# One core, two attention layers and two MLPs, forward and backward: chunks of wo kept over passes, 4 KiB transfers, gradient products in four row groups, and zero writes between the backward loads

## The chip, the cores and the metric

The kernel runs on one core of one Trainium2 chip. The metric is the device time of one execution in microseconds (us), as a median of several executions. Each profile, and each stage time read from one, is of a single execution of its kernel. A ratio is the mean time of one kernel's runs over the mean of the other's of the same rounds, so it is not quite the ratio of the medians quoted beside it.

Engines in the profile: PE does matrix products, PEld is its weight load (it overlaps PE), DVE and ACT evict results from PSUM (the memory that PE's products go to) to SBUF (the working memory), POOL and SP issue transfers. "Chunk" below is one piece of a weight matrix, 128 partitions by 2048 (or 1792) bf16 numbers, about 0.5 MB, loaded into a ring of streaming buffers.

## The reference

One token, decode, batch 1, all in bf16: four layers A1, B2, A3, B4 with residuals. A and B are used twice with the same weights.

```python
def A(x):   # attention over the last 4096 of 32768 cached keys
    q = (x @ wq).reshape(1, 1, 32, 128)               # wq 1024 x 4096
    p = softmax(q @ k[last 4096] * 128**-0.5)         # 4 kv heads, 8 q heads each
    return (p @ v[last 4096]).reshape(1, 1, 4096) @ wo # wo 4096 x 1024
def B(x):   # MLP with mish
    return mish(x @ w1 + b1) @ w2                     # w1 1024 x 3584, w2 3584 x 1024
x = x + A(ln(x)); x = x + B(ln(x)); x = x + A(ln(x)); x = x + B(ln(x))
# outputs: x, and the gradients of x, k_cache, v_cache, wq, wo, w1, b1, w2
```

Three facts matter. Every weight of wo, w1 and w2 is read in each of the four passes that need it, forward as it is stored, backward transposed, and the transposes are made on PE. The gradients of the weights are sums of two outer products (two layers), so each is a product with a contraction of only 2. And the gradients of the two caches are zero outside the last 4096 positions: 56 MB of zeros must be written some time.

## The kernel before

Weights wq, K and V stay in SBUF; wo, w1 and w2 are streamed. SP issues loads and zero writes in program order; a load waits only for its buffer. All other engines are ordered at build time by a scheduler. The backward stream of the MLP, with seven buffers:

```python
NB = 7
strm = tile_pool(name="strm", bufs=NB)
...
def mlp_bwd(g_col, g_bf, lname, sv):
    for c in reversed(range(TF // 2)):                  # 14 chunks of w2
        w = strm.tile([P, 2, D], BF16, name="w2_c", tag="st")     # cut: last ones held from forward
        nc.sync.dma_start(w[:], w2_v[:, 2 * c:2 * c + 2, :])      # 2 KB runs
        for tt in range(2):
            xpose_unit(w[:, tt, :], 8)    # 8 PE transposes to PSUM, one eviction back over w
        for tt in range(2):
            for dch in range(TD):
                mm(dacc[:, t:t + 1], w[:, tt, dch * P:(dch + 1) * P], g_bf[:, dch:dch + 1], ...)
    ...                                                 # the same with 16 chunks of w1
```

The zeros go out in 1 MB jobs: ten in each forward attention (`if c == NB - 1: zeros(10)` in the loop over wo), and in the backward in two blocks:

```python
g3, g3b = mlp_bwd(gcol, gcol_bf, "B4", sB4)
g2, g2b = attn_bwd(g3, g3b, "A3", sA3, True)
zeros(16)
g1, g1b = mlp_bwd(g2, g2b, "B2", sB2)
g0, g0b = attn_bwd(g1, g1b, "A1", sA1, False)
zeros(100)                                              # what is left
```

The gradients come last. Columns are transposed to rows on PE, and a transfer from the POOL queue puts each row in the tile ROWS. One product, one eviction:

```python
to_row(sB4["a_bf"], TF, 96, 0, "a4") ; to_row(...) x3    # 4 row puts before each gradient
def dw_tall(base, r0, L, out_v, name):
    for rr in range(2):
        for i in range(2):
            mm(ps[:], ROWS[base:base + 2, ...128 columns], ROWS[base:base + 2, ...512 columns],
               True, True, tile_position=(base, 0))     # all of one gradient in one row group
            ev_out(st[:, rr, i * 512:(i + 1) * 512], ps[:])
    nc.gpsimd.dma_start(out_v[:, r0:r0 + 2, :], st[:])
```

Of the kernel before, what the change touches and what calls it, by code (L numbers as in the profile page):

```python
# [15 lines left out]
P = 128  # L16
# [3 lines left out]
NB = 7  # L20
# [4 lines left out]
def kernel(  # L25
# [44 lines left out]
    stage = ctx.enter_context(tc.tile_pool(name="stage", bufs=4))  # L70
    pt = ctx.enter_context(tc.tile_pool(name="pt", bufs=4, space=bass.MemoryType.PSUM))
    pbig = ctx.enter_context(tc.tile_pool(name="pbig", bufs=1, space=bass.MemoryType.PSUM))
    pacc = ctx.enter_context(tc.tile_pool(name="pacc", bufs=1, space=bass.MemoryType.PSUM))

# [21 lines left out]
    ZC = 512  # L96
# [8 lines left out]

    wq_v = A_wq.rearrange("(t p) j -> p t j", p=P)
    wo_v = A_wo.rearrange("(t p) d -> p t d", p=P)
    w1_v = B_w1.rearrange("(t p) f -> p t f", p=P)
    w2_v = B_w2.rearrange("(t p) d -> p t d", p=P)
# [5 lines left out]
    for out_t in (out_2, out_3):  # L115
        for g in range(G):
            zflat = out_t[0, g, 0:ZR, :].rearrange("(p r) d -> p (r d)", p=P)
            for i in range(per // (8 * ZC)):
                zero_jobs.append(zflat[:, i * 8 * ZC:(i + 1) * 8 * ZC].rearrange("p (r c) -> p r c", c=ZC))

    def zeros(n):
        for _ in range(min(n, len(zero_jobs))):
            nc.sync.dma_start(zero_jobs.pop(0), zt[:, None, :].to_broadcast([P, 8, ZC]))
# [11 lines left out]
    def xpose_unit(ap2d, nb):  # L135
        ps = pt.tile([P, 8, P], BF16, name="tps", tag="pt")
        for b in range(nb):
            nc.tensor.transpose(ps[:, b, :], ap2d[:, b * P:(b + 1) * P], ident_bf[:])  # L138
        evac(ap2d, ps[:, 0:nb, :].rearrange("p b c -> p (b c)"), 0.08 * nb, 0.12 * nb)

# [6 lines left out]
    def ln_fwd(x_col, name):  # L147
# [14 lines left out]
        n_bf = keep.tile([P, TD], BF16, name=f"nbf_{name}")  # L162
        nc.vector.tensor_scalar(out=n_bf[:], in0=x_col[:], scalar1=s12[:, 0:1], scalar2=rstd[:, 0:1], op0=ALU.subtract, op1=ALU.mult)
# [4 lines left out]
    def ln_bwd(dn_ps, n32, rstd, g_col, name):  # L168
# [14 lines left out]
        g_bf = keep.tile([P, TD], BF16, name=f"gbf_{name}")  # L183
        nc.vector.tensor_copy(g_bf[:], g_new[:])
# [17 lines left out]
    def xpose_kv(lst):  # L202
        for w in lst:
            flat = w[:].rearrange("p t d -> p (t d)")
            for u in range(TK // 8):
                xpose_unit(flat[:, u * 1024:(u + 1) * 1024], 8)

# [34 lines left out]
    def to_kpart(src, name):  # L242
# [3 lines left out]
        dst = work.tile([P, TJ, P], BF16, name="kpart")  # L246
# [3 lines left out]
    def attn_fwd(x_col, lname, first):  # L250
# [40 lines left out]
        o_bf = keep.tile([P, HQ], BF16, name=f"obf_{lname}")  # L291
        nc.vector.tensor_copy(o_bf[:], oacc[:])
        sv["o_bf"] = o_bf
        yacc = acc_tile(TD)
        for c in range(HQ // 2):
            w = strm.tile([P, 2, D], BF16, name="wo_c", tag="st")
            nc.sync.dma_start(w[:], wo_v[:, 2 * c:2 * c + 2, :])
            if c == NB - 1:
                zeros(10)
# [11 lines left out]
    def mlp_fwd(x_col, lname, last):  # L311
# [3 lines left out]
        for t in range(TD):  # L315
            for hf in range(2):
                w = strm.tile([P, F // 2], BF16, name="w1_c", tag="st", padded_shape=[P, 2048])
                nc.sync.dma_start(w[:], w1_v[:, t, hf * (F // 2):(hf + 1) * (F // 2)])
                for b in range(TF // 2):
                    fb = hf * (TF // 2) + b  # L320
                    mm(hacc[:, fb:fb + 1], w[:, b * P:(b + 1) * P], n_bf[:, t:t + 1], t == 0 and fb == 0, t == TD - 1)
# [13 lines left out]
        a_bf = keep.tile([P, TF], BF16, name=f"abf_{lname}")  # L335
        nc.vector.tensor_mul(a_bf[:], h[:], t_f[:])
        sv["a_bf"] = a_bf
        yacc = acc_tile(TD)
        for c in range(TF // 2):
            w = strm.tile([P, 2, D], BF16, name="w2_c", tag="st")  # L340
            nc.sync.dma_start(w[:], w2_v[:, 2 * c:2 * c + 2, :])
# [23 lines left out]
    def mlp_bwd(g_col, g_bf, lname, sv):  # L365
        sv["g_bf"] = g_bf
        dacc = acc_tile(TF)
        for c in reversed(range(TF // 2)):
            w = w2_held.pop(c, None)
            if w is None:  # L370
                w = strm.tile([P, 2, D], BF16, name="w2_c", tag="st")
                nc.sync.dma_start(w[:], w2_v[:, 2 * c:2 * c + 2, :])
# [8 lines left out]
        dh_bf = keep.tile([P, TF], BF16, name=f"dhbf_{lname}")  # L381
        nc.vector.tensor_copy(dh_bf[:], dh[:])
# [3 lines left out]
        for t in range(TD):  # L386
            for hf in range(2):
                w = strm.tile([P, F // 2], BF16, name="w1_c", tag="st", padded_shape=[P, 2048])
                nc.sync.dma_start(w[:], w1_v[:, t, hf * (F // 2):(hf + 1) * (F // 2)])
                for u in range(2):  # L390
                    xpose_unit(w[:, u * 896:(u + 1) * 896], 7)
# [3 lines left out]
        return ln_bwd(nacc[:], sv["n32"], sv["rstd"], g_col, lname)  # L395
# [8 lines left out]
    def attn_bwd(g_col, g_bf, lname, sv, first):  # L404
        sv["g_bf"] = g_bf
        dacc = acc_tile(HQ)
        for c in range(HQ // 2):
            w = strm.tile([P, 2, D], BF16, name="wo_c", tag="st")
            nc.sync.dma_start(w[:], wo_v[:, 2 * c:2 * c + 2, :])
            for tt in range(2):  # L410
                xpose_unit(w[:, tt, :], 8)
# [4 lines left out]
        pad, rep = pad_cols(dacc[:], 1.0, f"do_{lname}")  # L416
# [19 lines left out]
        dq_bf = keep.tile([P, HQ], BF16, name=f"dqbf_{lname}")  # L436
        nc.scalar.activation(dq_bf[:], qacc[:], ACT.Copy, scale=scale)
# [6 lines left out]
        return ln_bwd(nacc[:], sv["n32"], sv["rstd"], g_col, lname)  # L444

    ROWS = keep.tile([P, 5120], BF16, name="ROWS")

    def to_row(col_bf, n, part, off, name):
        ps = pt.tile([HQ, P], BF16, name="rw", tag="pt")
        nc.tensor.transpose(ps[0:n, :], col_bf[:, 0:n], ident_bf[:])  # L450
        rt = work.tile([HQ, P], BF16, name="rt", tag="rt", bufs=4)
        nc.vector.tensor_copy(rt[0:n, :], ps[0:n, :])
        nc.gpsimd.dma_start(ROWS[part:part + 1, off:off + n * P].rearrange("o (n p) -> o n p", p=P), rt[0:n, :])

    def col_out(col_bf, n, out_flat, name):
        ps = pt.tile([HQ, P], BF16, name="rw", tag="pt")
        nc.tensor.transpose(ps[0:n, :], col_bf[:, 0:n], ident_bf[:])
        rt = work.tile([HQ, P], BF16, name="rt", tag="rt", bufs=4)
        nc.vector.tensor_copy(rt[0:n, :], ps[0:n, :])
        nc.gpsimd.dma_start(out_flat.rearrange("(n p) -> n p", p=P), rt[0:n, :])  # L460

    oq = [0]

    def dw_psum(n=512):
        return pt.tile([P, 512], FP32, name="ops", tag="pt")
# [4 lines left out]
    def dw_wide(base, t, lo, width, nfree, out_ap, name):  # L470

        st = stage.tile([P, width], BF16, name="st_w", tag="so", padded_shape=[P, 2048])
        for i in range(width // nfree):
            ps = dw_psum()
            mm(ps[:, 0:nfree], ROWS[base:base + 2, t * P:(t + 1) * P], ROWS[base:base + 2, 1024 + lo + i * nfree:1024 + lo + (i + 1) * nfree],
               True, True, tile_position=(base, 0))
            ev_out(st[:, i * nfree:(i + 1) * nfree], ps[:, 0:nfree])
        nc.gpsimd.dma_start(out_ap, st[:])

    def dw_tall(base, r0, L, out_v, name):  # L480

        st = stage.tile([P, 2, D], BF16, name="st_t", tag="so")
        for rr in range(2):
            for i in range(2):
                ps = dw_psum()
                mm(ps[:], ROWS[base:base + 2, (r0 + rr) * P:(r0 + rr + 1) * P], ROWS[base:base + 2, L + i * 512:L + (i + 1) * 512],
                   True, True, tile_position=(base, 0))
                ev_out(st[:, rr, i * 512:(i + 1) * 512], ps[:])
        nc.gpsimd.dma_start(out_v[:, r0:r0 + 2, :], st[:])  # L489

    def dkv(x3, y3, x1, y1, out_t):
        ov = out_t[0, :, Sk - W:, :].rearrange("g (p t) d -> p g t d", p=P)
        for c in range(NC):
            for gp in range(2):
                st = stage.tile([P, 2, TJ, DH], BF16, name="st_kv", tag="so")
                for j2 in range(TJ // 2):
                    ps = dw_psum()
                    for jj in range(2):
                        j = 2 * j2 + jj
                        mm(ps[:, jj * 256:(jj + 1) * 256], x3[32 * c:32 * c + 32, j * P:(j + 1) * P],  # L500
                           y3[32 * c:32 * c + 32, 2 * gp:2 * gp + 2, :].rearrange("p g d -> p (g d)"), True, False, tile_position=(32 * c, 0))
                        mm(ps[:, jj * 256:(jj + 1) * 256], x1[32 * c:32 * c + 32, j * P:(j + 1) * P],
                           y1[32 * c:32 * c + 32, 2 * gp:2 * gp + 2, :].rearrange("p g d -> p (g d)"), False, True, tile_position=(32 * c, 0))
                    ev_out(st[:, :, 2 * j2:2 * j2 + 2, :].rearrange("p g t d -> p t g d"),
                           ps[:].rearrange("p (t g d) -> p t g d", t=2, g=2))
                nc.gpsimd.dma_start(ov[:, 2 * gp:2 * gp + 2, c * TJ:(c + 1) * TJ, :], st[:])


    x1, sA1 = attn_fwd(x0, "A1", True)
    b1_f = load_col(B_b1, TF, "b1")  # L510
    gcol = load_col(grad_out[0, 0, :], TD, "gcol")
    gcol_bf = keep.tile([P, TD], BF16, name="gcolb")
    nc.vector.tensor_copy(gcol_bf[:], gcol[:])
    x2, sB2 = mlp_fwd(x1, "B2", False)
    x3, sA3 = attn_fwd(x2, "A3", False)
# [3 lines left out]
    col_out(x4_bf, TD, out_0[0, 0, :], "o0")  # L519


    g3, g3b = mlp_bwd(gcol, gcol_bf, "B4", sB4)
    g2, g2b = attn_bwd(g3, g3b, "A3", sA3, True)
    zeros(16)
    g1, g1b = mlp_bwd(g2, g2b, "B2", sB2)
    g0, g0b = attn_bwd(g1, g1b, "A1", sA1, False)
    col_out(g0b, TD, out_1[0, 0, :], "o1")
    zeros(100)


    to_row(sB4["a_bf"], TF, 96, 0, "a4")
    to_row(sB2["a_bf"], TF, 97, 0, "a2")
    to_row(sB4["g_bf"], TD, 96, 4096, "g4")
    to_row(sB2["g_bf"], TD, 97, 4096, "g2")
    for t in range(0, TF, 2):
# [63 lines left out]
```

## Time and profile before

Median 654 us in three runs (653.41 to 654.88). The boundaries below are read from PE's timeline: forward ends where PE transposes the output, the backward parts end at their layernorm product (the first one of each), the gradients start with the last of these.

| stretch, us | before |
|---|---|
| forward: A1, B2, A3, B4 end at | 98.5, 138.4, 188.4, 225.6 |
| backward: B4, A3, B2, A1 end at | 272.6, 351.0, 403.7, 453.4 |
| end of the profiled span | 652.0 |

The page's row of 40 slices (16.3 us each; digits are tenths, PEclk is the TensorE clock granted, GB/s what the transfers moved):

```profile
PE   3564034465444599889978888866376979999696
...
PEclk9985555555555599989975999995555555555555
...
GB/s 307 425 415 383 388 286 390 388 386 383 388 387 392 252 281 333 296 283 382 382 390 153 289 288 298 304 384 382 384 390 195 289 185 309 218 195 139 153 224 292
```

Forward (slices 1 to 14) the transfers run mostly at 383 to 425 GB/s and PE is half idle: bound by DMA. In the backward streams (slices 15 to 28) PE is at 0.6 to 0.9, the clock mostly full, and the transfers move about 290 GB/s except where zeros fill in: bound by PE and its evictions. In the gradients (from slice 29) the clock is half and PE is busy again.

Busy time by windows. The columns are the window, its length, busy us (and count) of PE, PEld, DVE, ACT, POOL, then clock, DMA share and GB/s. The rows are B2 forward, the B4 backward, resident transposes, dV and dK:

```profile
99.00:138.00 39.00, 16.59 (x449) 14.24 (x449) 3.40 (x21) 0.72 (x3) 0.00 (x0) 0.50 1.04 393
...
226.00:270.00 44.00, 40.97 (x865) 36.66 (x864) 22.59 (x37) 22.46 (x24) 0.66 (x1) 0.96 0.84 288
...
303.00:329.00 26.00, 26.00 (x470) 26.00 (x468) 23.23 (x37) 22.23 (x24) 0.00 (x0) 1.00 1.09 383
...
561.00:585.00 24.00, 23.71 (x124) 16.30 (x125) 10.73 (x22) 9.38 (x16) 5.72 (x8) 0.50 0.48 175
587.00:612.00 25.00, 24.58 (x128) 16.74 (x128) 11.20 (x22) 9.80 (x17) 5.72 (x8) 0.50 0.44 160
```

And a piece of PE's timeline in the backward stream (start, duration, what, and in brackets an idle time before it, if any):

```profile
246.50 0.35 PE L145 MATMUL acc<-gcolb,w_c 128*128 128x1 bf16 x8
246.72 0.44 PE L138 MATMUL tps<-ident_bf,w_c 128*128 128x128 bf16 x5
246.99 0.34 PE L145 MATMUL acc<-gcolb,w_c 128*128 128x1 bf16 x8
247.20 0.66 PE L138 MATMUL tps<-ident_bf,w_c 128*128 128x128 bf16 x9
```

The transposes (tps) of one chunk and the products (acc) of the chunk ahead of it alternate in pieces of 5 to 9 and 8. While one chunk's transposes are evicted, PE has another chunk's work. No idle time is marked.

Before the gradients PE waits for rows (the list of PE's waits from 400 us on: total, times, longest):

```profile
PE ops L145 <- DMA ROWS<-rt: 26.3, 4, 10.8
```

### The profile page before, as it was taken

What the parts mean: (1) busy time and instruction counts of PE and PEld (TensorE: products, weight loads), DVE (VectorE), ACT (ScalarE), POOL (GpSimd) and SP (SyncE); (2) the same over time, 40 slices, a digit from 0 to 9 for tenths busy, and PEclk for the clock granted to TensorE, in tenths of its full rate; (3) what the DMA queues carried; (4) which work ended last, traced back from release to release, by engine and by line L of the source; (5) the groups of instructions that cost most, each with busy time, mean ns of one, the idle gap of its engine ahead of it and who ended that gap; (6) DMA issues with size and microseconds to landing.
All of it is one profiled execution on the core that took longest, in us unless ns stands there. A gap on an engine that the chain in (4) does not pass through costs nothing. (4 is left out here: it accounts for less than half of the span.)

```text
span 652.0 us, 16240 instructions
## 1 busy us (share of the span) xinstructions
PE 451.2 (69%) x7117; PEld 325.0 (50%) x7117; DVE 242.1 (37%) x470; ACT 203.4 (31%) x292; POOL 62.3 (10%) x109
## 2 busy tenths in 40 slices
PE   3564034465444599889978888866376979999696
PEld 2444023353433497778967777746121323466431
DVE  1140000102001055546842454431254757644275
ACT  1030000000000055446821444420253747443274
POOL 0000000000000000000000000000233334322322
PEclk9985555555555599989975999995555555555555
DMA  8999999999999689989994889999995748553457
GB/s 307 425 415 383 388 286 390 388 386 383 388 387 392 252 281 333 296 283 382 382 390 153 289 288 298 304 384 382 384 390 195 289 185 309 218 195 139 153 224 292
DMA packets 118215, 205.10 MB, mean 315 GB/s; under 512 B 11514, under 2 KB 68992, under 8 KB 117120
## 3 DMA queue, kind: packets, MB, share of 16 engines
q1 hardware_dynamic: 107328, 164.13, 70.5%
q0 software_dynamic: 10816, 39.94, 16.0%
q8 instruction: 55, 0.90, 0.5%
q14 instruction: 16, 0.13, 0.1%
HBM read 105.39 MB, written 98.58 MB: 313 GB/s over the span
## 5 line engine op out<-in xcount | busy, mean ns | idle before, releaser
L145 PE MATMUL ops<-ROWS 2*128 2x512 bf16 (+1 forms) x248 | 104.8, 606 | 29.8 <-DMA ROWS<-rt 26.3
L145 PEld LDWEIGHTS <-w_c 128*128 128x128 bf16 x1792 | 60.2, 101 | 67.3 <-DMA w_c<-in_B_w_dram 40.5
L145 PEld LDWEIGHTS <-ROWS 2*128 2x128 bf16 x248 | 33.6, 137 | 99.7 <-issue 88.9
L138 PE MATMUL tps<-ident_bf,w_c 128*128 128x128 bf16 x896 | 72.1, 225 | 0.0
L133 ACT COPY w_c<-tps 128x896 bf16<-128x896 bf16 (+1 forms) x48 | 45.8, 955 | 79.7 <-PE tps L138 74.6
L145 PEld LDWEIGHTS <-wo_c 128*128 128x128 bf16 x1024 | 33.3, 101 | 63.8 <-DMA wo_c<-in_A_wo_dram 45.0
L130 DVE COPY w_c<-tps 128x1024 bf16<-128x1024 bf16 (+1 forms) x72 | 47.0, 656 | 46.1 <-PE tps L138 35.2
L138 PEld LDWEIGHTS <-w_c 128*128 128x128 bf16 x896 | 54.1, 100 | 0.1
L133 ACT CAST st_t<-ops 128x512 bf16<-128x512 f32 x63 | 35.8, 587 | 50.0 <-PE ops L145 43.3
L130 DVE CAST st_t<-ops 128x512 bf16<-128x512 f32 x57 | 39.0, 691 | 28.3 <-PE ops L145 21.5
L130 DVE CAST st_w<-ops 128x448 bf16<-128x448 f32 (+1 forms) x60 | 39.5, 658 | 21.1 <-PE ops L145 19.0
L133 ACT CAST st_w<-ops 128x448 bf16<-128x448 f32 (+1 forms) x68 | 37.1, 560 | 29.0 <-PE ops L145 27.1
L138 PE MATMUL tps<-ident_bf,wo_c 128*128 128x128 bf16 x512 | 39.9, 223 | 0.0
L130 DVE COPY wo_c<-tps 128x1024 bf16<-128x1024 bf16 x38 | 26.2, 692 | 28.9 <-PE tps L138 23.4
L133 ACT COPY wo_c<-tps 128x1024 bf16<-128x1024 bf16 x26 | 26.3, 1012 | 33.6 <-PE tps L138 29.8
L159 ACT ACTIVATE lnv<-var,eps_t 128x1 f32<-128x1 f32 x4 | 1.2, 295 | 107.0 <-DVE var L156 54.8
L130 DVE CAST st_kv<-ops 128x512 bf16<-128x512 f32 x30 | 20.8, 692 | 28.5 <-PE ops L145 26.1
L145 PE MATMUL acc<-obf_A_787,wo_c 128*128 128x1 bf16 x256 | 8.5, 166 | 32.8 <-DMA wo_c<-in_A_wo_dram 30.9
L138 PEld LDWEIGHTS <-wo_c 128*128 128x128 bf16 x512 | 30.4, 99 | 0.0
L133 ACT CAST st_kv<-ops 128x512 bf16<-128x512 f32 x34 | 19.9, 586 | 31.9 <-PE ops L145 30.7
L489 POOL DMA_DIRECT2D out_dram<-st_t x30 | 21.6, 720 | 44.8 <-ACT st_t L133 31.2
L145 PE MATMUL ops<-do3x,p_A_1983 32*128 32x256 bf16 x64 | 23.7, 414 | 0.8 <-DVE do3x L213 0.8
(442 smaller groups left out, 594.5 us busy)
## 6 DMA issues: line engine op xcount, KB each, us to landing
out_dram<-zt SPq DMA_DIRECT2D x56, 1024.0 KB, 10.8
wo_c<-in_A_wo_dram SPq DMA_DIRECT2D x64, 512.0 KB, 7.2
w_c<-in_B_w_dram SPq DMA_DIRECT2D x64, 448.0 KB, 5.6
w_c<-in_B_w_dram SPq DMA_DIRECT2D x49, 512.0 KB, 8.3
out_dram<-st_t POOLq DMA_DIRECT2D x30, 512.0 KB, 3.5
out_dram<-st_kv POOLq DMA_DIRECT2D x16, 512.0 KB, 4.0
out_dram<-st_w POOLq DMA_DIRECT2D x16, 512.0 KB, 3.3
out_dram<-st_w POOLq DMA_DIRECT2D x16, 448.0 KB, 2.8
```

Of the source, the lines that this page charges most:

```text
L130: nc.vector.tensor_copy(out_ap, in_ap)
L133: nc.scalar.copy(out_ap, in_ap)
L138: nc.tensor.transpose(ps[:, b, :], ap2d[:, b * P:(b + 1) * P], ident_bf[:])
L145: nc.tensor.matmul(out_ap, lhsT=lhsT, rhs=rhs, start=start, stop=stop, skip_group_check=True, **kw)
L159: nc.scalar.activation(lnv[:], var[:], ACT.Ln, bias=eps_t[:, 0:1], scale=1.0)
L489: nc.gpsimd.dma_start(out_v[:, r0:r0 + 2, :], st[:])
```

## The change

It has four intents. (1) Eight of the sixteen wo chunks stay in SBUF from the first pass on: two for good, six until the A3 backward ends. To pay for it the streaming ring has four buffers, not seven, and the staging tiles are allocated only when the six chunks are freed. (2) The large loads, the zero writes and the weight gradients move runs of 4 KiB (w1: 3.5) by giving each partition a pair of neighbouring rows; the vectors o and dO have to be permuted to match. (3) Most zeros leave the forward (14 jobs of 0.5 MB stay, where 20 of 1 MB were): one job is issued in each step of the backward streams. (4) A gradient's four 512-column products take their rows from four different row groups of PE (blocks of 32 partitions, chosen by `tile_position`); dV and dK from two; six PSUM slots instead of four.

```diff
-NB = 7
+NB = 4
+NR = 2
+NE = 6
-    wo_v = A_wo.rearrange("(t p) d -> p t d", p=P)
+    wo_v = A_wo.rearrange("(c p t) d -> c p t d", p=P, t=2)
+    def wo_chunk(c, last=False):            # cut: returns a kept chunk, or loads one
+        if c < NR + NE and not wo_kept.get("closed"):
+            w = (keep if c < NR else hold).tile([P, 2, D], BF16, name=f"wo_k{c}")
+        else:
+            w = strm.tile([P, 2, D], BF16, name="wo_c", tag="st")
 ... in attn_fwd
-            if c == NB - 1:
-                zeros(10)                   # of 1 MB
+            if c == z_at:
+                zeros(nz)                   # 6 and 8, of 0.5 MB
 ... in mlp_bwd (w2, w1) and in attn_bwd (wo), after each load
+            zeros(1)
 ... gradients
+    def outer(R, q, lo, ro, nf, ps):
+        mm(ps[:, 0:nf], R[32 * q:32 * q + 2, 0, lo:lo + P], R[32 * q:32 * q + 2, 1, ro:ro + nf],
+           True, True, tile_position=(32 * q, 0))
+                for q in range(4):
+                    ps = dw_psum()
+                    outer(R, q, (2 * c0 // 4) * P, i * 512, 512, ps)
+                    pss.append(ps)
+                for q in range(4):
+                    ev_out(sts[q // 2][:, q % 2, i * 512:(i + 1) * 512], pss[q])
-    col_out(db1_bf, TF, out_7, "o7")
+    nc.gpsimd.dma_start(out_7.rearrange("(c p t) -> p c t", p=P, t=2), ...)   # 4-byte runs
```

## The prediction

> **What bounds it now (654 us).** Three regimes, from the 40-slice row and busy time by windows.
> (1) Forward, 0 to 226 us: DMA-bound. DMA share is 1.0 or more, 384 to 391 GB/s with 2 KB runs (wo, w2), 399 with w1's 3.5 KB, 422 with wq's 4 KB. The timeline shows a wo or w2 chunk every 1.36 us, a wq chunk every 1.24. Ten 1 MB zero writes stand in front of nine wo loads in both attention layers; PE waits 24.4 us for one of those loads in A1.
> (2) Backward, 226 to 455: the three weight streams of each pass run at PE/eviction pace (PE 85% busy, 1.5 to 1.7 us a chunk, DMA only 290 to 330 GB/s). Between them lie 28 us of transposing resident weights and two 23 us attention chains. Zeros (16 MB, then 20 MB) fill mostly just these.
> (3) Gradients, 455 to 648: bound by 0.43 us per two-row matmul (clock 0.5; 64 take 27.6 us). DVE needs 0.69 us and ACT 0.59 us per 128x512 eviction, so both together about 20.5 us for 64. Gaps of 5 to 12 us wait for ROWS.
>
> **What the change does.**
> - Forward: 13.6 MB of zeros and 4.2 MB of wo go; 4 KB runs save 0.12 us a chunk. A first-in-first-out estimate of DMA, buffers and PE, which gives the old stage ends within 2%, gives x1 near 73 us (was 96) and forward end about 30 us earlier.
> - Backward: 92 zero writes of 0.5 MB now stand one before each next load. Estimated from the 4 KB rate, a zero costs 1.22 us, a pair 2.36 to 2.46 us, against 1.5 to 1.7 us of PE pace: the streams become DMA-bound. Loads (39 MB) plus zeros (48 MB) need about 205 us; the streams took 154. Only four buffers and no block of zeros leave DMA idle for about 45 us in the transposes and attention of A3, and again in A1. Backward: +52 us.
> - Gradients: four row groups should overlap. The Trainium skill ("TensorE: Matmul & The Clock Gate", Part 3, measured speedup) gives 3.07x for four row tiles; this trace shows only column groups overlapping (four 512-column matmuls each 0.21 us at full clock). Then eviction and the four staging buffers bind (two filled and sent together). Estimated w2 28.5 to 22.5, w1 24.5 to 22, wo 27.6 to 25.5, wq 27.4 to 23.5, each K/V gradient 25 to 16: -34 us. But each row put costs Pool 0.52 us, and there are 16 or 24 before each stage instead of 4, queued behind the last output: +25 us. Net -9.
> - Small: two extra transpose chains, +2 us each; bias gradient in 4-byte runs, a few us.
>
> **Sum.** 654 - 30 + 52 - 9, with a few us of give and take: about 664 us, range 640 to 688. Faster 0.12, same 0.45, slower 0.43.
>
> **What would show it.** Right: x4 near 195 us; backward stream slices at 400 GB/s or more with PE about half busy; low-GB/s slices in A3's transposes; gradients starting near 478; PE waiting 11 to 16 us for row tiles before w1, wo, wq; matmuls in row groups starting under 0.2 us apart. Wrong: streams at 1.7 us a chunk; gradient stages at DMA rate.
>
> **What would make it wrong.** Mixed loads and zero writes running above 440 GB/s (up to 20 us faster) or slower for turning direction. The clock falling to half in the starved streams: the scheduled order there is all transposes, then all products of one chunk, so eviction is exposed; up to 50 us slower. Row groups not overlapping: 30 us slower. Interleaved weight columns loading slowly: 10 us slower.

## The result

The changed kernel takes 722.67 us (720.30 to 725.32, four runs) against 654.48 in the same rounds: ratio 1.105, 95% interval 1.100 to 1.109. It is correct, and slower. The predicted 664 us and its range up to 688 are missed.

| stretch, us | before | after | difference | predicted |
|---|---|---|---|---|
| forward | 225.6 | 208.4 | -17 | -30 |
| backward: B4 | 47.0 | 84.9 | +38 | |
| A3 | 78.4 | 87.3 | +9 | |
| B2 | 52.7 | 90.0 | +37 | |
| A1 | 49.7 | 67.4 | +18 | |
| backward in all | 227.7 | 329.7 | +102 | +52 |
| gradients to the end | 198.6 | 185.6 | -13 | -9 |
| span | 652.0 | 723.6 | +72 | +13 |

(The prediction's three terms add to +13; with some give and take it said 664.) The sum of the gradients came near the prediction, by terms that cancelled (see below). The forward gained too little, and the backward lost twice what was expected. The row of slices, now 18.1 us each:

```profile
PE   3564334563367788988987766778675464878364
...
PEclk9985555555565555757965555555555555555555
...
GB/s 317 418 415 408 292 335 372 180 160 326 342 283 396 341 364 374 387 301 167 3 3 240 394 218 354 384 339 346 229 3 151 259 166 242 231 269 249 184 169 296
```

Slices 13 to 16 are the B4 backward: PE is 0.7 to 0.8 busy, but the clock is half, where before it was full, and the transfers move 341 to 396 GB/s. In A3's resident transposes and attention (slices 20 and 21) they move nearly nothing. Windows of B2 forward, B4 backward, the resident transposes, dV and dK:

```profile
76.00:121.00 45.00, 16.98 (x450) 14.55 (x450) 3.60 (x23) 0.72 (x3) 0.00 (x0) 0.50 0.96 346
...
226.00:286.00 60.00, 47.74 (x620) 40.90 (x621) 16.33 (x26) 16.76 (x19) 0.00 (x0) 0.50 1.00 360
...
331.00:361.00 30.00, 30.00 (x506) 30.00 (x505) 24.82 (x39) 23.41 (x25) 0.00 (x0) 0.94 0.12 45
...
642.50:659.00 16.50, 13.75 (x126) 8.54 (x128) 10.16 (x21) 9.29 (x18) 5.00 (x8) 0.50 0.70 240
660.50:676.00 15.50, 13.14 (x126) 9.42 (x128) 10.19 (x21) 8.39 (x16) 5.69 (x8) 0.50 0.70 230
```

In the B4 backward PE ran 620 instructions (products and transposes) in 60 us at half clock, where before it ran 865 in 44 us. PE's timeline shows how. The first lines are the moment at which the old order ends, the later ones are the steady state in w1:

```profile
214.74 0.34 PE L170 MATMUL acc<-gB_pair,w_c 128*128 128x1 bf16 x8
...
216.68 1.07 PE L155 MATMUL tps<-ident_bf,w_c 128*128 128x128 bf16 x16 [0.39 <-DMA w_c<-in_B_w_dram]
218.45 0.56 PE L170 MATMUL acc<-gB_pair,w_c 128*128 128x1 bf16 x16 [0.70 <-ACT w_c L150]
219.96 1.89 PE L155 MATMUL tps<-ident_bf,w_c 128*128 128x128 bf16 x16 [0.96 <-DMA w_c<-in_B_w_dram]
...
425.78 1.65 PE L163 MATMUL tps<-ident_bf,w_c 128*128 128x128 bf16 x14
427.64 0.38 PE L170 MATMUL acc<-dh_pair,w_c 128*128 128x1 bf16 x8 [0.20 <-DVE w_c L147]
428.37 0.32 PE L170 MATMUL acc<-dh_pair,w_c 128*128 128x1 bf16 x6 [0.36 <-ACT w_c L150]
428.55 1.65 PE L163 MATMUL tps<-ident_bf,w_c 128*128 128x128 bf16 x14
```

All 16 (or 14) transposes of a chunk stand in one block and all its products in the next, so PE waits for its own evictions. Sixteen transposes took 1.07 us at 216.68 and 1.89 us at 219.96: the clock fell to half between them, after two waits for DMA with an eviction wait in between, and it stayed there. In steady state one chunk takes 428.55 - 425.78 = 2.77 us. The listing of PE's order in the built programs says that it is so by construction. Both programs start the stream alike, then part (T are transposes, M are products, in number):

```
before: ... T11 M8 T5  M8  T9  M8  T11 M8  T4  M8  T11 M8 T5 ...
after:  ... T11 M8 T1 M16 T16 M16 T16 M16 T16 M16 T16 M16 T16 ...
```

No line of the change sets PE's order. The scheduler, which places PE's instructions, placed them differently when a zero write stood between two loads on SP; with the zeros taken out again it returned to the mixed order (next section). Where a chunk needs no load (the ones held from the forward, the kept wo in A3), the changed program stays mostly mixed, although a zero write is issued with each of these too.

PE's waits for row tiles are 7 to 12 us each, for w1 and wo shorter than the predicted 11 to 16:

```profile
PE ops L170 <- DMA Rq<-rt: 13.4, 3, 12.4
PE ops L170 <- DMA Ro<-rt: 8.4, 1, 8.4
PE ops L170 <- DMA R_8239<-rt: 8.1, 3, 7.3
PE ops L170 <- DMA R_8022<-rt: 7.1, 1, 7.1
```

One more line of that timeline stands out, a single late weight in the w1 stream of B2:

```profile
437.23 1.68 PE L163 MATMUL tps<-ident_bf,w_c 128*128 128x128 bf16 x14 [5.81 <-DMA w_c<-in_B_w_dram]
```

### The profile page after: what moved, and what is told of

It is laid out like the page before. It is cut to its first block, busy times and chain, and to the rows that moved or that the text cites. A ratio compares the mean times of both kernels' runs of the same rounds, so it can differ in the third digit from the quotient of the medians.

```text
span 723.6 us, 16229 instructions
## 1 busy us (share of the span) xinstructions
PE 470.8 (65%) x7092; PEld 352.3 (49%) x7092; DVE 236.4 (33%) x468; ACT 199.8 (28%) x294; POOL 89.8 (12%) x173
## 5 line engine op out<-in xcount | busy, mean ns | idle before, releaser
L170 PEld LDWEIGHTS <-w_c 128*128 128x128 bf16 x1792 | 61.1, 105 | 106.6 <-DMA w_c<-in_B_w_dram 56.2
L150 ACT COPY w_c<-tps 128x1024 bf16<-128x1024 bf16 (+1 forms) x52 | 47.3, 909 | 163.0 <-PE tps L155 89.2
L163 PE MATMUL tps<-ident_bf,w_c 128*128 128x128 bf16 x448 | 52.9, 311 | 5.8 <-DMA w_c<-in_B_w_dram 5.8
L155 PE MATMUL tps<-ident_bf,w_c 128*128 128x128 bf16 x448 | 49.2, 296 | 5.8 <-DMA w_c<-in_B_w_dram 5.8
L163 PEld LDWEIGHTS <-w_c 128*128 128x128 bf16 x448 | 45.2, 144 | 5.9 <-DMA w_c<-in_B_w_dram 5.9
L155 PEld LDWEIGHTS <-w_c 128*128 128x128 bf16 x448 | 42.5, 138 | 6.2 <-DMA w_c<-in_B_w_dram 6.1
L170 PE MATMUL acc<-nB_pair,w_c 128*128 128x1 bf16 x448 | 16.7, 166 | 28.1 <-DMA w_c<-in_B_w_dram 25.0
L170 PE MATMUL acc<-a_pair,w_c 128*128 128x1 bf16 x448 | 16.2, 166 | 27.4 <-DMA w_c<-in_B_w_dram 23.0
L170 PE MATMUL acc<-dh_pair,w_c 128*128 128x1 bf16 x448 | 21.5, 168 | 16.4 <-ACT w_c L150 11.2
L170 PE MATMUL acc<-gB_pair,w_c 128*128 128x1 bf16 x448 | 19.4, 167 | 12.9 <-ACT w_c L150 9.1
L170 PE MATMUL ops<-Rq 2*128 2x512 bf16 x42 | 17.2, 586 | 14.5 <-DMA Rq<-rt 13.4
L170 PE MATMUL ops<-Ro 2*128 2x512 bf16 x44 | 18.1, 587 | 10.8 <-DMA Ro<-rt 8.4
L170 PE MATMUL acc<-gA_pair,wo_c 128*128 128x1 bf16 x352 | 16.3, 168 | 13.2 <-ACT wo_c L150 10.2
```

What stands on the lines that cost most here:

```text
L150: nc.scalar.copy(out_ap, in_ap)
L155: nc.tensor.transpose(ps[:, b, :], ap2d[:, b * P:(b + 1) * P], ident_bf[:])
L163: nc.tensor.transpose(ps[:, b, :], ap2d[:, o:o + 2 * P - 1:2], ident_bf[:])
L170: nc.tensor.matmul(out_ap, lhsT=lhsT, rhs=rhs, start=start, stop=stop, skip_group_check=True, **kw)
```

## The experiments

Theory 1: the backward is slow because a zero before each load makes it DMA-bound (this was predicted), and because PE's order became serial and its clock half (named in the prediction only as a risk). Rivals: four streaming buffers starve the stream; the new layout costs; other parts of the change do it. The expectations split theory 1: up to dummy_fill, "theory 1" there is PE's order and clock alone and "theory 2" is the loads held up by the zero writes; in six_bufs, theory 1 is both and theory 2 the buffers.

The numbers of the fifteen experiments follow in the order in which they ran, below the two kernels compared; in each group of runs the old kernel ran beside them. All but one_row_group are correct. "Backward" is the time from the end of the forward to the last layernorm of the backward.

| kernel | median, us | ratio to before | forward ends | backward |
|---|---|---|---|---|
| before | 654 | 1 | 225.6 | 227.7 |
| after | 722.67 | 1.105 | 208.4 | 329.7 |
| zero_blocks | 691.38 | 1.059 | 206.2 | 265.8 |
| pipelined | 723.2 | 1.106 | 208.3 | 327.2 |
| serial_no_zeros | 773.21 | 1.182 | 206.3 | 349.1 |
| before_zeros_between | 715.36 | 1.093 | 206.9 | 319.0 |
| pipelined_forced | 704.98 | 1.080 | 209.2 | 315.2 |
| dummy_fill | 702.58 | 1.074 | 206.8 | 304.8 |
| six_blocks | 651.47 | 0.996 | 194.9 | 240.4 |
| rows_on_sp | 725.49 | 1.111 | 206.7 | 326.1 |
| one_row_group | 756.02 | 1.153 | 209.8 | 326.7 |
| bias_runs | 719.25 | 1.099 | 209.3 | 323.8 |
| six_rows | 633.43 | 0.969 | 194.3 | 238.4 |
| best | 590.17 | 0.900 | 196.5 | 248.4 |
| six_bufs | 702.53 | 1.071 | 196.4 | 318.8 |
| six_fill | 677.44 | 1.037 | 193.9 | 295.2 |
| after_peorder | 741.23 | 1.133 | 208.8 | 344.8 |

### zero_blocks: the zeros out of the streams

```diff
-            zeros(1)      # all three places in the backward streams
     g2, g2b = attn_bwd(g3, g3b, "A3", sA3, True, "B2")
+    zeros(32)             # one block, as before; the rest after the last layer
```

> The changed kernel without the zero writes between backward loads: 32 of them (16.8 MB) in one block behind the A3 backward pass, as before, the rest at the end. The scheduled matmul order goes back to mixing one chunk's transposes with the neighbour's products. Both theories expect a gain: theory 1 (serial order of transposes and products per chunk, made by the build-time scheduler because of the zeros, and the half clock that follows) and theory 2 (loads held up by the zero writes at the DMA engines) expect 1.5 to 1.8 us a backward chunk, backward near 235 us instead of 331, and, with the zeros now competing in the gradient part, 635 to 655 us in all. Theory 1 also expects a granted clock near 1.0 in the streams.

It took 691.38 us. The backward fell by 64 us and the listing of PE's order is mixed again (T4 M8 T15 M8 T2 M8 T15 ...), with the clock at 0.95 in B4:

```profile
226.00:262.00 36.00, 28.32 (x567) 23.87 (x565) 14.40 (x24) 15.08 (x17) 0.00 (x0) 0.95 0.85 253
```

So the zeros between the loads cause the serial order and most of the backward's loss. But 691 is far from the expected 635 to 655: this stream still moved only 253 GB/s, and PE waited for DMA. Something else binds, which six_blocks found.

### pipelined: an order written in the source

```diff
             xpose_unit(w[:, tt, :], 8)
-        (products of this chunk)
+        pend.append((c, w)); if len(pend) > 1: (products of the chunk before)
```

> The changed kernel with all zeros left between the loads, but the products of a chunk written after the transposes of the next one, so that PE never waits for the eviction of the chunk that it just transposed. Theory 1 (order and clock): chunk pace falls from 2.8 to 3.0 us to the DMA pair's 2.4 to 2.5 us, the clock in the streams rises towards 1.0, backward 331 to about 285 us, total 670 to 690 us. Theory 2 (zero writes hold up the loads): no change, 715 to 725 us.

It took 723.2 us, no change, but the test is void: the scheduler moved the products back behind their own transposes. The PE timeline shows 8 and 8 products around each block of 16 transposes and the same wait for ACT. PE's order has to be fixed too; pipelined_forced does that.

### serial_no_zeros: the serial order without zeros

zero_blocks, with PE kept in program order, which is all transposes, then all products of a chunk:

```diff
-    ctx.enter_context(tc.manual_schedule(engines={ET.SP}))
+    ctx.enter_context(tc.manual_schedule(engines={ET.SP, ET.PE}))
```

> zero_blocks with PE held to program order, which is the same serial order (16 transposes, then the 16 products of the same chunk) as in the changed kernel, but no zero writes between the loads. Theory 1: the streams stay slow, 2.4 to 3.0 us a chunk with a clock near 0.5, total 690 to 720 us, 50 us or more above zero_blocks. Theory 2: as fast as zero_blocks, within 10 us.

It took 773.21 us. This one edit costs 82 us over zero_blocks. The B4 backward:

```profile
226.00:286.00 60.00, 48.06 (x622) 40.96 (x620) 16.68 (x27) 16.41 (x19) 0.00 (x0) 0.50 0.56 169
```

PE's columns are nearly those of the changed kernel in the same window (47.74 us, 620 products, clock 0.50), while the transfers move 169 GB/s instead of 360. A stream with the serial order runs at this pace with or without zeros.

### before_zeros_between: only the zeros, in the old kernel

```diff
+            zeros(1)      # 0.5 MB, after each backward load of the old kernel
-    zeros(16)
```

> The old kernel (seven buffers, 2 KiB runs, nothing kept, single row group) with only this part of the change: 0.5 MB zero writes between the backward loads, and 10 MB fewer in the forward pass. The scheduled order becomes serial per chunk here too. Both theories expect backward streams near 2.8 to 3.0 us a chunk; forward 25 us shorter, backward 90 us longer, total 690 to 730 us. If instead the buffers, the runs or the strided transposes of the changed kernel are the cause, it stays near 640 us.

It took 715.36 us, as expected, with none of the other parts of the change and with seven buffers:

```profile
226.00:286.00 60.00, 48.23 (x613) 40.92 (x611) 17.51 (x33) 15.81 (x17) 0.00 (x0) 0.50 1.06 397
```

Layout, kept wo and row groups are cleared: one zero per load alone raises the backward from 228 to 319 us. It also shortened the forward by 19 us, because fewer zeros are left there: a gain as large as the 17 us of the change needs neither kept chunks nor longer runs.

### pipelined_forced: products one chunk late, order fixed

The edits of pipelined and of serial_no_zeros together, on the changed kernel.

> The edit of pipelined again, with PE held to program order, because the build-time scheduler had moved the products back behind their own chunk's transposes, so that run tested nothing. All zeros stay between the loads. Theory 1 (serial order, PE waiting for evictions at half clock): a chunk costs PE 16 transposes of 0.107 and 16 products of 0.036 us, 2.3 us, even at half clock, below the DMA pair's 2.45; the streams run at 2.4 to 2.6 us a chunk instead of 2.8 to 3.0, backward 290 to 305 us instead of 331, total 685 to 700 us. Theory 2 (zeros hold up the loads): no gain, 720 us.

It took 704.98 us, just above the expected 685 to 700. The PE waits in 226 to 286 us changed their kind:

```profile
PE tps L163 <- DMA w_c<-in_B_w_dram: 8.2, 12, 1.6
PE tps L155 <- DMA w_c<-in_B_w_dram: 6.7, 6, 2.7
```

Evictions no longer hold PE; the loads do, and the clock is 0.59. A stream whose loads come late loses its clock too. The transfers moved 368 GB/s here, against 416 in dummy_fill (next) with the same loads and zeros, so their full rate was not what held the loads back; a buffer that is held one chunk longer would explain it, which no run tested.

### dummy_fill: more work for PE

On the changed kernel with PE in program order, two useless 512-column products in each chunk, one before each half of its products:

```diff
+    def fill():
+        mm(dum["t"][:, 0:512], ident_bf[:], K_t[0]...[:, 0:512], True, True)
             for tt in range(2):
+                fill()
                 for dch in range(TD):
                     mm(dacc[:, t:t + 1], ...)
```

> The changed kernel in its own serial order (PE held to program order), with two useless 512-column matmuls per backward chunk in the two places where PE waits for an eviction. They add PE work, 0.85 us a chunk at half clock, 0.43 at full. If the clock gate falls because PE waits (theory 1), it now stays near 1.0 and the chunk falls from 2.9 to 2.0 to 2.5 us in spite of the added work, total 670 to 695 us. If the clock has another cause, the chunk grows to 3.0 to 3.6 us, total 730 to 790 us.

It took 702.58 us: with work added, 20 us less than the changed kernel. The window, and the stream on PE's timeline:

```profile
226.00:286.00 60.00, 48.43 (x783) 34.67 (x783) 20.25 (x38) 18.69 (x21) 0.00 (x0) 1.00 1.03 416
```

```profile
242.24 0.96 PE L163 MATMUL tps<-ident_bf,w_c 128*128 128x128 bf16 x14
243.04 0.38 PE L170 MATMUL big<-K,ident_bf 128*128 128x512 bf16 x1
244.01 0.35 PE L170 MATMUL acc<-dh_pair,w_c 128*128 128x1 bf16 x8 [0.60 <-ACT w_c L150]
244.23 0.38 PE L170 MATMUL big<-K,ident_bf 128*128 128x512 bf16 x1
244.44 0.29 PE L170 MATMUL acc<-dh_pair,w_c 128*128 128x1 bf16 x6
244.59 0.95 PE L163 MATMUL tps<-ident_bf,w_c 128*128 128x128 bf16 x14
```

The clock is 1.00, 14 transposes take 0.95 us instead of 1.65, and a chunk takes 244.59 - 242.24 = 2.35 us, which is at the lower end of the predicted 2.36 to 2.46 us: now the stream is DMA-bound, at 416 GB/s. The share of PE that counts as busy is the same as in the changed kernel (48 of 60 us). At half clock each item takes longer, so the busy share looks healthy while PE does less: 620 instructions in these 60 us in the changed kernel, 783 here, and 865 in 44 us before.

### after_peorder: the control for dummy_fill

PE in program order on the changed kernel, nothing else.

> The changed kernel with PE kept in program order and nothing else: the control for dummy_fill. In its backward streams the build already places all transposes of a chunk and then all its products, which is program order, so if the useless products (the clock) made dummy_fill's 20 us, this control stays at 715 to 730 with the clock at 0.50 in the first backward MLP. If the fixed order made them, it falls to about 703.

It took 741.23 us, above the expected 715 to 730, with the clock at 0.50 in the first backward MLP:

```profile
226.00:286.00 60.00, 48.18 (x631) 41.34 (x630) 17.03 (x27) 16.14 (x19) 0.00 (x0) 0.50 0.99 353
```

The fixed order is no gain but a loss of 19 us, 11 of them in A3, where the changed kernel still had some freedom. So dummy_fill's gain is the clock's: 40 us of backward against this control, 25 us against the changed kernel.

### six_blocks, six_bufs and six_fill: the buffers

Each takes its base kernel and gives two of the kept wo chunks to the ring:

```diff
-NB = 4
-NR = 2
+NB = 6
+NR = 0
```

six_blocks is zero_blocks with this edit, six_bufs the changed kernel, six_fill dummy_fill.

> zero_blocks (691 us) with six stream buffers instead of four; paid for with the two wo chunks kept to the end (six instead of eight are kept). If the round trip of four buffers bounds the forward MLP parts (45 us instead of 42) and the backward streams of zero_blocks (B2 backward 70 us instead of 53), forward comes down by 8 to 15 us and backward by 25 to 40 us: 640 to 660 us in all. If not, 685 to 695 us.

> The changed kernel with six streaming buffers (paid for by two fewer kept wo chunks), zeros between the loads as before. Theory 1 (the streams are slow because one zero precedes each load and because the order is serial at half clock): forward ends 10 to 12 us earlier as in six_blocks, backward stays at 320 to 335 us, in all 705 to 715. Theory 2 (four buffers starve the backward streams): backward falls by 40 us or more, in all below 680.

> dummy_fill (useless products that keep the clock up) with six streaming buffers. If the 25 us by which dummy_fill's backward exceeds a DMA-bound estimate come from four buffers, the backward falls from 306 to about 285 us and the whole to 670 to 680. If not, the backward stays within 6 us of 306 and the whole is 685 to 695, the forward alone being 11 us shorter.

six_blocks took 651.47 us, 40 less than zero_blocks: 11 in the forward, 25 in the backward, the rest after. The B2 forward, to be compared with 45 us at 346 GB/s in the changed kernel and 39 at 393 in the old one:

```profile
76.00:117.00 41.00, 17.44 (x452) 15.01 (x452) 3.82 (x25) 0.72 (x3) 0.00 (x0) 0.50 1.01 391
```

An estimate of why: a load lands about 5.5 us after its issue (medians 5.3 and 5.6 of the whole run in the list of transfers of the changed kernel) and a chunk's transfer lasts some 1.25 us (0.52 MB at 416 GB/s), so four transfers (5.0 us) do not cover the round trip and six (7.5 us) do. With six, the forward ends at 194.9 us, where the prediction had put it for four.

six_bufs took 702.53 us, just under the expected 705: forward 12 us earlier, backward 11 us shorter, far from the 40 of the rival theory. six_fill took 677.44, inside the 670 to 680 expected if buffers made it all, but its backward fell 10 us, to 295, not to 285: between the two expectations. So buffers are worth 10 us in the DMA-bound backward and 12 in the forward, and much more (25) where the zeros don't hide it.

### rows_on_sp: row puts from another queue

```diff
-                nc.gpsimd.dma_start(R[32 * q + lay:...
+                nc.sync.dma_start(R[32 * q + lay:...
```

> The changed kernel with one edit: the 80 small row puts before the gradient parts go out from the SP queue, idle then, instead of the Pool queue behind the output writes. If those puts are the price of the four row groups (PE waits 7 to 12 us before each part, and outputs queue behind them), 20 to 35 us come off: 690 to 703 us. If the waits have another cause, above 715 us.

It took 725.49 us: the hoped gain is missed, and the other branch (above 715) holds. PE still waits:

```profile
PE ops L170 <- DMA R<-rt: 19.6, 5, 8.9
PE ops L170 <- DMA Rq<-rt: 11.9, 5, 9.1
PE ops L170 <- DMA Ro<-rt: 7.9, 3, 7.2
```

The queue was not the limit. The rows are made by a PE transpose and a DVE copy that stand behind the preceding gradient, so no queue can put them earlier. That reading was tested by six_rows.

### one_row_group: do the row groups overlap?

Wrong (the profile is of interest, not the result): all products of a set read the rows of the first group.

```diff
-        mm(..., R[32 * q:32 * q + 2, 0, ...], R[32 * q:32 * q + 2, 1, ...], ..., tile_position=(32 * q, 0))
+        mm(..., R[0:2, 0, ...], R[0:2, 1, ...], ..., tile_position=(0, 0))
```

> The changed kernel with every gradient product of a set of four (two for dV and dK) read from one and the same row group, timing only: its results are wrong on purpose, for all four take the first group's rows. Theory A (products in different row groups overlap, and that is what shortened the gradient parts): w2, w1, wo and wq go back to 27 to 29 us of PE time each from 24 to 28, dV and dK to about 25 us each from 16; the whole 22 to 35 us above the changed kernel's 723 (745 to 758). Theory B (they do not overlap; the parts got shorter by the finer evictions, more PSUM buffers and row puts): within 5 us of 723.

It took 756.02 us, as theory A expected. The parts for wo, dV and dK:

```profile
619.60:650.00 30.40, 28.22 (x64) 8.51 (x64) 18.82 (x29) 16.52 (x32) 9.37 (x18) 0.50 0.58 231
651.70:675.00 23.30, 23.30 (x125) 16.20 (x126) 10.59 (x20) 9.09 (x16) 4.82 (x7) 0.50 0.52 178
677.00:701.00 24.00, 23.90 (x125) 16.55 (x126) 10.78 (x21) 9.19 (x17) 5.70 (x8) 0.50 0.52 173
```

In the changed kernel dV and dK take about 17 and 16 us with PE busy for 13 to 14, and wo takes 25.6 (PE's timeline, 616.07 to 641.65). The row groups overlap, and are worth 33 us in all. What binds next is eviction. The Trainium skill ("TensorE: Matmul & The Clock Gate", Part 3, "Measured speedup vs the span model") gives 3.07x for four row tiles; for wo the part shortened by 30.7 / 25.6 = 1.20 only (the window above leaves out its last 0.3 us). The skill's page "TensorEngine Tiling (Array Packing)" ("PSUM Bottleneck") says that after the speedup the copy from PSUM may become the bottleneck; in the row-group version DVE is busy for 18.7 and ACT for 16.8 of wo's 25.6 us, and PE's remaining waits there name both.

### bias_runs: the 5.8 us stall

```diff
-    nc.gpsimd.dma_start(out_7.rearrange("(c p t) -> p c t", p=P, t=2), db1_bf...)   # 4-byte runs
+    (two PE transposes to [14, 128, 2])
+    nc.gpsimd.dma_start(out_7.rearrange("(c q) -> c q", q=2 * P), rt7...)           # 512-byte runs
```

> The changed kernel with the bias gradient transposed on PE and written in 14 runs of 512 bytes instead of 1792 runs of 4 bytes. If the one 5.8 us stall of the backward stream near 437 us (weights landing late) is caused by this write, the stall goes and the whole is 5 to 7 us shorter: 715 to 719. If the stall has another cause, 721 to 725.

It took 719.25 us, ratio 1.099 against 1.105. The 5.8 us wait is gone from PE's list, while rows_on_sp (5.4 us) and one_row_group (5.8), which keep the 4-byte write, still have it; in the changed kernel the write was issued at 421.63 us and took 16.0, to just when the wait ended. In the total some 4 us arrived, as a difference of ratios from different rounds whose intervals overlap (1.094 to 1.103 against 1.100 to 1.109), so the size of the gain is only roughly known. The same 7 KB in the list of transfers (KB, then us from issue to landing), in the changed kernel:

```profile
out_dram<-db_bf POOLq DMA_DIRECT2D x1, 7.0 KB, 16.0
```

and in this one:

```profile
out_dram<-rt POOLq DMA_DIRECT2D x1, 7.0 KB, 3.2
```

The Trainium skill ("DMA: Bandwidth & Descriptors", "Specifications") puts the smallest transfer for line rate at 512 bytes; the two landing times, 16.0 and 3.2 us, agree in direction.

### six_rows: the rows made early

six_blocks, with the row tiles of w2, w1 and wo made before the A1 backward:

```diff
     g1, g1b = mlp_bwd(g2, g2b, "B2", sB2, "A1")
+    R2 = new_rows("R2"); rows_put(R2, 0, "a", ...); ...    # and R1, Ro
     g0, g0b = attn_bwd(g1, g1b, "A1", sA1, False, "X0")
```

> six_blocks with the row tiles of the w2, w1 and wo gradients made before the last attention backward (their data are ready then) instead of just before each part. In six_blocks PE waits 7 to 19 us for row tiles at each of these three parts, so if the late making of the rows is what costs (the reading after rows_on_sp gained nothing by another queue), the gradient part shrinks by 20 to 30 us: 622 to 632 in all. If the row puts themselves slow the streams as much as they save, 645 to 652.

It took 633.43 us, 18 less than six_blocks; 20 to 30 were expected. Of PE's waits for rows from 400 us on, only one is left:

```profile
PE ops L170 <- DMA Rq<-rt: 13.7, 3, 12.7
```

### best: all that helped

six_rows, plus: wq's rows right after the last layer, the streaming ring reused as output staging, bias_runs, and the zeros placed where the profile of six_blocks showed idle transfers:

```diff
-    x3, sA3 = attn_fwd(x2, "A3", False, 8)
+    x3, sA3 = attn_fwd(x2, "A3", False, 22)
-    zeros(32)                              # after the A3 backward
+            if lname == "B2" and c == TF // 2 - NB:
+                zeros(46)                  # after the first six loads of the B2 backward
-    stage = tile_pool(name="stage", bufs=4)
+    stage = strm
```

> Not the change any more: six_blocks with early rows (those of wq right after the last attention backward), the weight buffers reused as output staging, 22 zero writes placed in A3's forward attention, 46 after the first weights of the second backward MLP, 36 at the end instead of 66, and the bias gradient in 512-byte runs. From six_blocks' 651: 25 for the rows, 5 for the bias write, 15 to 25 for zeros that move from the gradients part into stretches where the DMA moves under 75 GB/s: 595 to 615. If zeros placed there delay the loads behind them, 615 to 630.

It took 590.17 us (587.39 to 591.22), ratio 0.900 (0.897 to 0.903) to the old kernel, correct, and a little better than expected. It waits for no rows:

```profile
PEclk9996555555555699998995679959755555555555
GB/s 296 414 420 407 389 329 392 396 407 417 369 377 405 137 340 290 298 160 371 416 415 416 403 207 284 301 145 223 387 410 415 357 363 334 314 352 253 282 364 283
```

Zero writes fill slices that were idle. B4's stream, with no zero between two of its loads, keeps its clock (0.93 in 196 to 246 us); B2's starts at 0.61 (324 to 340), where the 46 zeros stand between its loads, and ends at 1.00 (352 to 381). Its parts were not tried one by one beyond six_blocks, bias_runs and six_rows.

## Why the prediction was wrong

**Backward, +52 predicted, +102 measured: the failed step.** The prediction's sentence is "a zero costs 1.22 us, a pair 2.36 to 2.46 us, against 1.5 to 1.7 us of PE pace: the streams become DMA-bound". It took the old PE pace as given. What the runs showed instead is that the zeros also changed PE's order to the serial one, that the clock fell to half, and that PE's own cycle became 2.77 us in w1, above the DMA's. The risk stood in the prediction's last paragraph, with "up to 50 us slower", but outside its sum and its range. The 102 us, split by differences of the backward column, where the order of taking things away matters and each is a difference of two profiled runs:

- half clock: 329.7 - 304.8 = 25 us (after against dummy_fill; 40 against the control with the same fixed order); the profile of after is the slowest of its four executions and that of dummy_fill the fastest, and with the backward of rows_on_sp (326.1), whose source is the same there, it is 21,
- four instead of six buffers: 304.8 - 295.2 = 10 us (dummy_fill against six_fill),
- DMA-bound pairs and the rest: 295.2 - 227.7 = 67 us (six_fill against before).

The last holds the predicted term, 52, and is 15 larger. The bias write explains at most some 3 of these (the longest wait for a weight that six_fill still has in that stream is 2.9 us). six_fill also carries the useless products and the fixed order, which cost 11 us in A3 at half clock (after_peorder). None of this was measured apart, so the 15 stay open.

**Why the clock fell.** The Trainium skill ("TensorE: Matmul & The Clock Gate", Part 1, "What's actually happening") says that the throttled clock is the default and that activity releases it. The trace agrees: clock 0.50 in the serial stream, 1.00 when two more products per chunk fill part of its gaps (dummy_fill). That the serial order brings the half clock, without any zeros, is shown by serial_no_zeros; that the half clock slows the serial stream is shown by dummy_fill. Why the build's scheduler changes PE's order when zeros stand between loads is not shown; that it does is shown by the listings and by zero_blocks.

**Forward, -30 predicted, -17 measured.** The step was the estimate of DMA, buffers and PE that "gives the old stage ends within 2%". It was fitted on seven buffers and carried to four. A1 came almost as predicted (75.9 us against 73), and A3 gained 8 us more. But B2 and B4 took 45 us each, where they had taken 40 and 37 with seven buffers: +13 us, back in time with six (six_blocks). The right mechanism, the wrong round trip of a buffer: that the ring is what costs is measured, the round trip is the estimate above.

**Gradients, -9 predicted, -13 measured: near, but partly by luck.** Two of its terms were off and cancelled. The six parts went from 158 us (the prediction's own readings) to about 136, so -22 instead of -34, and the waits for rows from 26 us to 37, so +11 instead of +25. w2 and wo came as predicted (22.5 and 25.6 us), as did dV and dK (about 17 and 16), but w1 took 28.5 us instead of 22 and wq 26.7 instead of 23.5; why these two did not shorten was not tested. That the row groups overlap is shown by one_row_group. Why the rows are late was wrongly read at first as a queue of puts on POOL (rows_on_sp); their making, behind the part before, is what six_rows removed.

**DMA idle in A3's transposes: right.** 45 GB/s in that window against 383 before.

## What to carry to other kernels

When a change moves transfers only, still compare the built order of every engine that a scheduler places, in the streams that matter: here one more kind of transfer between the loads on the DMA queue turned a mixed PE order into a serial one. Don't carry a pace over into a stream that the change starves: a half clock hides behind a healthy busy share, so read the granted clock and the number of instructions in the window. Put filler transfers in blocks where the transfers idle, after enough loads that the next stream starts at once (best did both; neither was tested alone), and size a ring by the landing time over the pace before giving its memory away.

## What the Trainium skill lacked or had wrong

- "TensorE: Matmul & The Clock Gate", Part 1, describes waits for DMA of several us as what drops the clock. It also mentions brief idling of PE between groups of products, in a kernel whose clock went back and forth, but no length of the gaps. It lacks the case of this kernel: gaps of 0.2 to 0.8 us in each chunk of 2.8 us went with a clock that stayed at 0.50 through 60 us with PE busy 80% of the time, and pure fill work made the kernel 20 us faster (dummy_fill; 39 us against the control of the same order).
- The same page, Part 4 (PE-mode transpose), says that the full clock does not engage for transposes in one kernel's context. As this kernel issues them, it does: 26.0 us of resident transposes ran at a clock of 1.00 before the change, and 30.0 us at 0.94 after.
- The same page, Part 3, gives 3.07x for four row tiles without a word on what a whole gradient part gains: 1.20x for wo here (30.7 to 25.6 us), where eviction binds next. The page on tiling does warn of it.
- "DMA: Bandwidth & Descriptors" gives 512 bytes as the limit, but not what one small transfer does to others: 7 KB in 4-byte runs landed after 16.0 us, and a weight load beside it came 5.8 us late.
- "Perfetto Trace Analysis" ("Identifying the Most-Contended Engine") says that the occupancy of the DMA engines misleads, but not by how much: their share was 1.00 at 360 GB/s in the changed kernel and 1.03 at 416 GB/s with the same transfers in dummy_fill, so a full share is not yet full rate.
